# Staging buffers of a filter's first stage moved into an idle region, eight for one stream and five for the others

## The chip, the cores and the metric

One core of a Trainium2 chip runs the whole program. The metric is the device time of one execution in microseconds (us), the median of several runs. The engines are PE (matmuls; its weight loads are a row of their own, PEld), DVE (vector), ACT (activations and copies), POOL and SP; SP does nothing here but issue DMAs, and ACT issues some as well.

## The reference, cut to what matters

Two branches read the same normalized input. A is a long convolution over the sequence, done by FFT; B is a gated feed-forward net.

```python
xn = layernorm(q)                                # 2048 x 512
# A: short causal filter over k, times v, then a long filter per channel
kv = (sum over t of k_pad[t:t+S] * shift_k[:, 3-t]) * v
y  = irfft(rfft(pad(kv)) * rfft(pad(ssm_k)))[:S] + kv * ssm_D
s  = xn * y
# B
h  = gelu(xn @ w_gate) * (xn @ w_up)             # 512 -> 1792
g  = silu(h @ w_down)                            # 1792 -> 512
out = q + s * g
```

## The kernel before

**The branches.** B goes in four row groups q = 0 to 3 of 512 rows. A group has 14 units m (L971): a gate matmul group `tg` and an up group `tu` of four 128x512 matmuls each, a gelu on ACT into GE (L986) and a product on DVE into HT (L989). The down-projection `down(q)` (L992) makes four tiles jt of 14 matmuls each; the first of them is cut into three pieces, so that it can begin before all of HT is there. A tanh on ACT (L1004) and a DVE instruction (L1006) turn each tile into the gate G. XN, the normalized input, is computed on DVE (`ln(q)`, L739, beginning with `bn_stats` at L742) and for q > 0 transposed by DMAs that SP issues (L764).

**The filter.** A's FFT of length 4096 is two stages of matmuls with tables of sines. Between the stages the data go through DRAM, because the second stage needs them in another order. The first stage (`stage1`, L877) makes 16 tiles for the filter's own taps (stream H, from HTr, the transposed `ssm_k`) and later 16 for the products kv (stream K, from V). Each tile is two matmuls into a pair of PSUM banks, a copy by ACT (L563) into a staging buffer of the tile AST, and a store: H to the DRAM tensor ZH, issued by ACT; K to ZK, issued by SP. When all of ZH is stored, the second stage of H (L912 to L920) loads it in 16 parts (BH), multiplies, copies through AST with a scale (L917) and stores to ZS. When all of ZK is stored, the main loop (L1027) loads BK from ZK and HS from ZS, transforms, multiplies with the filter on DVE (L1044), transforms back and stores to ZI; the last loop reads ZI (BI) and finishes. The kv products are made on DVE by `kshift(i)` (L936), nine instructions for each of four groups. A table for the way back is transposed by one DMA on SP (L1019) after the first stage of K.

**The buffers.** AST has three slots, which H's stage 1, K's stage 1 and H's stage 2 share, each with a DMA semaphore of its own:

```python
AST = new("AST", [128, 3, 2, 512], BF16)                 # L410
pAST = Pool_("AST", 3)                                   # L530
a = B(f"A{x}{t}", pAST)                                  # L879, and L913 for stage 2
```

G (16 KB per partition) is written by the tanh instructions only; at the start the same bytes hold Hn, the loaded `ssm_k`, and from 8 KB on the four BH slots lie over them. HTr ends where KK, the loaded `k`, begins (`kk_at`). HS and, at the end, BI lie over KK; HB, BO and BK lie over V and the scratch of `kshift`. PSUM has eight banks: at most four at a time go to B's tiles (pool `psF`), and at most three pairs to A's (pool `psC`).

**The order.** Nothing is ordered by hand. A planner (`Sched.run`, L307) places tasks on engines by a model of their durations: it takes the engine that can start first and, among the tasks that can start there within 0.25 us, the one with the lowest `prio`. Loads are an engine of their own in this model (`LOAD_BW`), and stores by ACT count as a fixed time after issue (`STORE`, L27; used in L892). `after=` makes a task follow others in the plan. The instructions are then issued in the planned order, each engine's in sequence, and each waits on semaphores for what it touches (`Trk`, L51). So an instruction whose data come later than planned holds up what is queued behind it on its engine, SP's DMA issues included. Of the priorities, a lower number going first: copies of H 2, stage 1 of K 3, stage 2 of H on PE 5 (its copies 2.5), up groups 9 + q, gate groups 10 + q, whole down tiles and last pieces 8.5 + q, first pieces 11.1 + q, `ln` 2 for group 1, `kshift` 4, stores 0, transposes of XN -1, BH loads 0.5.

Of the kernel before, what the change touches and what calls it, by code (L numbers as in the profile page):

```python
# [6 lines left out]
BF16 = mybir.dt.bfloat16  # L7
# [16 lines left out]
N_WARM = 16  # L24
ORDER = "w1 k0 v0 w2 k1 v1 w3 d0 d1 k2 v2 x1 k3 v3 x2 x3"
NF_BANKS = 4
STORE = 3500.0  # L27
NC_PAIRS = 3


# [20 lines left out]
class Trk:  # L51
# [313 lines left out]
def act(n, sb=False):  # L365
    return 170.0 + n * 0.833 + (30.0 if sb else 0.0)
# [6 lines left out]
def build_kernel(nc, A_q, A_k, A_v, A_shift_k, A_ssm_k, A_ssm_D, B_w_gate, B_w_up, B_w_down, out):  # L373
    with ExitStack() as es0:
# [8 lines left out]
        def at(name, shape, dt, offset):  # L383
            return nc.alloc_sbuf_tensor_at(name, shape, dt, offset=offset)
# [61 lines left out]
        ZK = nc.dram_tensor("ZK", [NG, 128, DM], BF16, kind="Internal")  # L446
# [25 lines left out]
        def bank(b):  # L472
            return PSALL[:, 512 * b.slot:512 * (b.slot + 1)]
# [4 lines left out]
        def R_bank(b):  # L478
            return [R_ps[b.slot // 2][b.slot % 2]]
# [15 lines left out]
        R_AST = [res(f"AST{j}", AST[:, j, :, :]) for j in range(3)]  # L495
# [57 lines left out]
        def op(engs, fn, r=(), w=(), rr=(), ww=(), prio=5, lat=0.0, after=()):  # L553

            def emit(e):
                R = rr() if callable(rr) else rr
                W = ww() if callable(ww) else ww
                trk.op(e, lambda h: fn(e, h), r=R, w=W)
            return S.add(engs, emit, r=r, w=w, prio=prio, lat=lat, after=after)

        def copy(e, h, o, i):
            if e == "ACT":
                return h.activation(o, i, ACTF.Copy)  # L563
            return h.tensor_copy(o, i)

        def mm(h, o, l, r, st, sp):
            return h.matmul(o, lhsT=l, rhs=r, start=st, stop=sp)  # L567
# [30 lines left out]

        ZERO = AST[:, 0, 0, :]
        bwarm = B("warm")  # L600
        S.add([("DVE", 250.0)], lambda e: trk.op("DVE", lambda h: h.memset(ZERO, 0.0), w=[R_AST[0]]), w=[bwarm], prio=-9)
        warm = B("pswarm", pF)

        def warm_up(e):
            for i in range(N_WARM):
                trk.op("PE", lambda h: mm(h, bank(warm), ZERO[:, 0:128], ZERO, True, True), r=[R_AST[0]], w=R_bank(warm), accum=True)
# [266 lines left out]


        s1_tasks = {"H": [], "K": []}

        def stage1(x, t, data, R_data, b_data, Z, prio):  # L877
# [8 lines left out]
            op([("ACT", act(1024))], lambda e, h: copy(e, h, AST[:, a.slot, :, :].rearrange("p c d -> p (c d)"), ps(psl(p))),  # L886
               r=[p], w=[a], rr=lambda: R_ps[psl(p)], ww=lambda: [R_AST[a.slot]], prio=prio)

            def st(e):
                dst = bass.AP(Z, 2 * t * DM, [[32 * DM, 128], [DM, 2], [1, DM]])  # L890
                dma(e, dst, AST[:, a.slot, :, :], d_ast[a.slot], [R_AST[a.slot]], [R_Z[x][t]])
            S.add([("ACT" if x == "H" else "SP", 350.0)], st, r=[a], w=[bZ[x][t]], prio=0, lat=STORE if x == "H" else 0.0, nbytes=262144 if x == "K" else 0)  # L892

        d_ast = [dsem(f"d_ast{j}") for j in range(3)]
# [4 lines left out]
        def z_pair(Z, n):  # L899
            return bass.AP(Z, 2 * n * 128 * DM, [[DM, 128], [128 * DM, 2], [1, DM]])  # L900

        def fwd(p, T, R_T, buf):
            def f(e):
                s = psl(p)
                for i in range(2):
                    trk.op("PE", lambda h, i=i: mm(h, ps(s, i), MT[:, 0, :], T[:, buf.slot, i, :], True, True),
                           r=[R_MT, R_T[buf.slot]], w=[R_ps[s][i]], accum=True)
            return f

        d_bh = [dsem(f"d_bh{j}") for j in range(4)]  # L910
        h2_tasks = []
        for n in range(16):  # L912
            bh, p, a = B(f"bh{n}", pBH), B(f"psf{n}", pC), B(f"hf{n}", pAST)  # L913
            S.add([("SP", 350.0)], lambda e, n=n, bh=bh: dma(e, BH[:, bh.slot, :, :], z_pair(ZH, n), d_bh[bh.slot], R_Z["H"], [R_BH[bh.slot]]),
                  r=bZ["H"], w=[bh], prio=0.5, nbytes=262144, after=h_tr_tasks)
            h2_tasks.append(S.add([("PE", pe(2))], fwd(p, BH, R_BH, bh), r=[bMT, bh], w=[p], prio=5, lat=200.0))
            op([("ACT", act(1024))], lambda e, h, p=p, a=a: h.activation(AST[:, a.slot, :, :].rearrange("p c d -> p (c d)"), ps(psl(p)), ACTF.Copy, scale=2.0 ** -12),  # L917
               r=[p], w=[a], rr=lambda p=p: R_ps[psl(p)], ww=lambda a=a: [R_AST[a.slot]], prio=2.5)
            S.add([("SP", 350.0)], lambda e, n=n, a=a: dma(e, ZS[n], AST[:, a.slot, :, :], d_ast[a.slot], [R_AST[a.slot]], [R_Z["S"][n]]),
                  r=[a], w=[bZ["S"][n]], prio=0, nbytes=262144)  # L920


        kshift_tasks = []
# [40 lines left out]

        for i in range(4):
            kshift(i)
        for t in range(NT):
            stage1("K", t, V[:, t, :], R_V[t], [bKV[t // 4]], ZK, 3)

# [22 lines left out]
        def down(q):  # L992
            for jt in range(4):
                p = B(f"psd{q}_{jt}", pF)
                t = 4 * q + jt

                for m0, m1 in ((0, 4), (4, 9), (9, 14)):
                    def f(e, p=p, jt=jt, m0=m0, m1=m1):
                        for m in range(m0, m1):
                            trk.op("PE", lambda h, m=m: mm(h, bank(p), HT[:, q % 2, m, 128 * jt:128 * (jt + 1)], Wd[:, m, :], m == 0, m == MF - 1),  # L1000
                                   r=[R_HT[q % 2][m], R_Wd[m // 7]], w=R_bank(p), accum=True)
                    down_tasks[q].append(S.add([("PE", pe(m1 - m0))], f, r=(bHT[q] if jt else bHT[q][m0:m1]) + bWd[m0 // 7:(m1 + 6) // 7], w=[p], prio=9 + q - 0.5 if jt or m1 == MF else 11.1 + q, lat=200.0))
                bt = B(f"tanh{q}_{jt}")
                op([("ACT", act(512))], lambda e, h, t=t, p=p: h.activation(G[:, t, :], bank(p), ACTF.Tanh, scale=0.5), r=[p], w=[bt],  # L1004
                   rr=lambda p=p: R_bank(p), ww=[R_G[t]], prio=1, after=h_tr_tasks + (h2_tasks if q >= 2 else []))
# [150 lines left out]
```

## Time and profile before

| | us |
|---|---|
| median of 3 runs (lowest, highest) | 236.66 (236.32, 240.0) |
| the profiled execution | 235.92 |
| its span in the trace | 234.1 |
| PE busy | 209.5 |
| DVE busy | 169.8 |
| ACT busy | 121.5 |

Spans start with the first and end with the last instruction of the trace, so a profiled execution's own time is a little longer. Busy time of PE is modelled: a matmul that stands alone counts 0.38 us, one in a full row far less, so the count of matmuls in a stretch says more than the busy share. Issuing a DMA does not count as busy time of the engine that issues it; the rows ACTq and SPq show it. In a timeline, a row has start, duration, engine, line, operation, result and source, count, and in brackets the idle time before it with what ended it.

### The profile page before, as it was taken

To read this page: it belongs to the slowest core of one execution; us is meant where nothing else is said; L and a number is where in the kernel's file an instruction comes from. 1 tells how busy PE (TensorE), PEld (TensorE's weight loads), DVE (VectorE), ACT (ScalarE), POOL (GpSimd) and SP (SyncE) were. 2 spreads that over 40 slices of the span, in tenths; PEclk is the share of its full clock that TensorE was granted. 3 is DMA by queue.
4 is the path that set the end of the run, shared out by engine and by line. 5 is a ranking of instruction groups with operands and counts; after the bars stand their busy time and mean duration, and the time that the engine had idled before them with its cause. 6 is when DMAs were issued, how large, how long until landed. Compare 5 with 4: busy or idle time off the path is not lost.

```text
span 234.1 us, 2865 instructions
## 1 busy us (share of the span) xinstructions
PE 209.5 (89%) x979; PEld 92.3 (39%) x996; DVE 169.8 (73%) x250; ACT 121.5 (52%) x154; POOL 16.8 (7%) x43
## 2 busy tenths in 40 slices
PE   7599977899996989999969899999999999999990
PEld 2355432234442333443334344444344444444440
DVE  6978875968696879894014798988894646989535
ACT  2698575667966688876163255553434623131220
POOL 8632000010300000001000000000000000000000
PEclk9999999999999999999999999999999999999996
DMA  6999999956788888699797989999972267703402
GB/s 170 393 294 365 372 387 414 416 210 188 230 197 254 282 278 298 226 269 320 148 250 223 304 269 296 294 305 303 293 217 90 90 236 233 251 8 114 152 0 90
DMA packets 47617, 56.96 MB, mean 243 GB/s; under 512 B 13809, under 2 KB 31986, under 8 KB 47602
## 3 DMA queue, kind: packets, MB, share of 16 engines
q1 hardware_dynamic: 45298, 52.58, 71.6%
q10 hardware_dynamic: 2304, 4.20, 4.7%
q8 instruction: 8, 0.13, 0.2%
q14 instruction: 7, 0.06, 0.1%
HBM read 35.26 MB, written 18.87 MB: 231 GB/s over the span
## 4 chain that ended last, share of the span: by engine, by line
PE 51%; DMA 27%; ACT 11%; SPq 6%; issue 2%; DVE 2%; ACTq 0%
PE psall L567 49%; DMA ZH<-AST 11%; DMA ZK<-AST 5%; ACT AST L563 5%; DMA Hn<-in_A_ssm_k_dram 4%; DMA ZS<-AST 3%; DMA ZI<-BO 3%; SPq L1019 2%; SPq L544 2%; ACT AST L917 2%; DMA BK<-ZK 2%; SPq L764 2%; ACT GE L986 1%; PE psall L800 1%; ACT BO L563 1%
## 5 line engine op out<-in xcount | busy, mean ns | idle before, releaser
L567 PE MATMUL psall<-xnT,Wu 128*128 128x512 bf16 x224 | 56.4, 379 | 1.3 <-ACT AST L563 1.1
L989 DVE TENSOR_TENSOR HT<-psall,GE 128x512 bf16<-128x512 f32 x56 | 37.9, 686 | 26.6 <-PE psall L567 24.4
L986 ACT ACTIVATE GE<-psall 128x512 bf16<-128x512 f32 x56 | 33.4, 598 | 45.5 <-PE psall L567 43.9
L567 PE MATMUL psall<-xnT,Wg 128*128 128x512 bf16 x224 | 56.1, 379 | 0.3 <-ACT GE L986 0.3
L567 PE MATMUL psall<-Wd,HT 128*128 128x512 bf16 x219 | 51.4, 379 | 2.7 <-ACT AST L917 2.4
L1044 DVE TENSOR_TENSOR HB<-psall,HS 128x1024 bf16<-128x1024 f32 x32 | 36.9, 1216 | 10.0 <-PE psall L567 10.0
L563 ACT ACTIVATE AST<-psall 128x1024 bf16<-128x1024 f32 x32 | 32.5, 1025 | 11.3 <-DMA ZH<-AST 5.9
L567 PEld LDWEIGHTS psall<-Wd,HT 128*128 128x128 bf16 x224 | 21.9, 98 | 29.0 <-ACT AST L917 2.8
L567 PEld LDWEIGHTS psall<-xnT,Wu 128*128 128x128 bf16 x224 | 21.3, 98 | 28.1 <-ACT AST L563 1.7
L567 PEld LDWEIGHTS psall<-xnT,Wg 128*128 128x128 bf16 x224 | 21.6, 98 | 26.9 <-ACT GE L986 1.2
L1006 DVE SCALAR_TENSOR_TENSOR G<-G,psall 128x512 bf16<-128x512 bf16 x16 | 10.5, 682 | 20.9 <-ACT G L1004 20.9
L563 ACT ACTIVATE BO<-psall 128x1024 bf16<-128x1024 f32 x16 | 16.4, 1023 | 14.5 <-PE psall L567 12.2
L917 ACT ACTIVATE AST<-psall 128x1024 bf16<-128x1024 f32 x16 | 16.2, 1026 | 10.6 <-DMA ZK<-AST 5.9
L1004 ACT ACTIVATE G<-psall 128x512 bf16<-128x512 f32 x16 | 9.4, 597 | 18.1 <-PE psall L567 18.0
L567 PE MATMUL psall<-HB,MT 128*128 128x512 bf16 x62 | 16.0, 380 | 1.0 <-ACT BO L563 0.8
L958 DVE TENSOR_TENSOR KTM<-KK,SKB 128x2048 bf16<-128x2048 bf16 x12 | 14.6, 1218 | 0.1
L960 DVE TENSOR_TENSOR KAC<-KAC,KTM 128x2048 bf16<-128x2048 bf16 x12 | 14.6, 1217 | 0.1
L567 PE MATMUL psall<-BH,MT 128*128 128x512 bf16 x32 | 9.5, 381 | 3.3 <-DMA BH<-ZH 2.1
L567 PE MATMUL psall<-HTr,F 128*128 128x512 bf16 x29 | 8.6, 381 | 3.6 <-ACT AST L563 3.5
L749 POOL TENSOR_TENSOR mv<-mv,NHALF 128x4 f32<-128x4 f32 x4 | 5.4, 1338 | 84.1 <-DVE mv L748 84.1
L742 DVE BATCH_NORM_STATS2 stats<-X 128x6 f32<-128x512 bf16 x16 | 10.4, 671 | 0.9 <-DMA X<-in_A_q_dram 0.9
L1084 DVE TENSOR_TENSOR XN<-psall,XN 128x1024 bf16<-128x1024 f32 x8 | 9.6, 1216 | 0.7 <-PE psall L567 0.7
(73 smaller groups left out, 139.8 us busy)
## 6 DMA issues: line engine op xcount, KB each, us to landing
ZH<-AST ACTq DMA_DIRECT2D x16, 256.0 KB, 5.6
ZK<-AST SPq DMA_DIRECT2D x16, 256.0 KB, 2.6
BH<-ZH SPq DMA_DIRECT2D x16, 256.0 KB, 3.5
ZS<-AST SPq DMA_DIRECT2D x16, 256.0 KB, 2.9
HS<-ZS SPq DMA_DIRECT2D x16, 256.0 KB, 5.4
HS<-ZS SPq DMA_DIRECT2D x32, 128.0 KB, 5.1
BK<-ZK SPq DMA_DIRECT2D x16, 256.0 KB, 4.8
ZI<-BO SPq DMA_DIRECT2D x16, 256.0 KB, 4.6
```

What stands on the lines that cost most here:

```text
L563: return h.activation(o, i, ACTF.Copy)
L567: return h.matmul(o, lhsT=l, rhs=r, start=st, stop=sp)
L742: op([("DVE", 670.0)], lambda e, h, t=t: h.bn_stats(stats[:, t, :], X[:, t, :]), r=[bX[q][t % 4 // 2]], w=[bst[t]], rr=[R_X[t]], ww=[R_st[ ...
L917: op([("ACT", act(1024))], lambda e, h, p=p, a=a: h.activation(AST[:, a.slot, :, :].rearrange("p c d -> p (c d)"), ps(psl(p)), ACTF.Copy, ...
L958: op([("DVE", dur)], lambda e, h, j=j, m=m: h.tensor_tensor(KTM[:, m.slot, :, :], kk(j), sk(j), ALU.mult), r=need + [bSKB, a], w=[m], rr=l ...
L960: op([("DVE", dur)], lambda e, h, m=m: h.tensor_tensor(KAC[:, a.slot, :, :], KAC[:, a.slot, :, :], KTM[:, m.slot, :, :], ALU.add), r=[m], ...
L986: op([("ACT", act(512))], lambda e, h: h.activation(GE[:, g.slot, :], bank(pg), ACTF.Gelu_apprx_tanh), r=[pg], w=[g], rr=lambda: R_bank(pg ...
L989: op([("DVE", dve(512, 1))], lambda e, h: h.tensor_tensor(HT[:, q % 2, m, :], bank(pu), GE[:, g.slot, :], ALU.mult), r=[pu, g], w=[bHT[q][m]],
L1004: op([("ACT", act(512))], lambda e, h, t=t, p=p: h.activation(G[:, t, :], bank(p), ACTF.Tanh, scale=0.5), r=[p], w=[bt], rr=lambda p=p: R_ ...
L1006: op([("DVE", dve(512, 1))], lambda e, h, t=t, p=p: h.scalar_tensor_tensor(out=G[:, t, :], in0=G[:, t, :], scalar=1.0, in1=bank(p), op0=AL ...
L1044: op([("DVE", dve(1024, 1))], lambda e, h, k=k, pk=pk, qq=qq, hs=hs: h.tensor_tensor(HB[:, qq.slot, :, :].rearrange("p c d -> p (c d)"), p ...
L1084: op([("DVE", dve(1024, 1))], lambda e, h, p=p, xs=xs: h.tensor_tensor(xs, ps(psl(p)), xs, ALU.mult), r=[p], w=[bS[j], bXN[2 * j], bXN[2 * ...
```

## The change

H's stage 1 gets eight staging slots of its own, ASH, laid over G. The three slots of AST and two new ones, ASX, are left to K's stage 1 and H's stage 2 together. ASX lies over 2 KB of HTr's end and 2 KB of KK's beginning; HS and BI move up by 2 KB, and HB, BO and BK down by 1 KB. The copies of H now follow the transposes of `ssm_k` (over whose source ASH lies), the copies of K follow H's stage 1 and the first `kshift`, and the tanh instructions follow the ZH stores. `STORE` goes from 3500 to 5000 ns. H's stage 2 stands behind `kshift` in the source, its BH loads follow the ZH stores, and its matmuls' priority goes from 5 to 10.5. The first pieces of the down-projection go from 11.1 + q to 10.05 + q. No work is added or taken away; the rest of the kernel is unchanged.

```diff
-STORE = 3500.0
+STORE = 5000.0
...
-        HS = at("HS", [128, 4, 2, 2, DM], BF16, kk_at)
-        place["at"] = kk_at + 19456
+        ASX = at("ASX", [128, 2, 2, DM], BF16, kk_at - 2048)
+        ASH = at("ASH", [128, 8, 2, DM], BF16, g_at)
+        HS = at("HS", [128, 4, 2, 2, DM], BF16, kk_at + 2048)
+        place["at"] = kk_at + 18432
...
-        BI = at("BI", [128, 8, 2, DM], BF16, kk_at)
+        BI = at("BI", [128, 8, 2, DM], BF16, kk_at + 2048)
+        ast = {"H": [ASH[:, j, :, :] for j in range(8)], "K": [AST[:, j, :, :] for j in range(3)] + [ASX[:, j, :, :] for j in range(2)]}
...
-        pAST = Pool_("AST", 3)
+        pAST = {x: Pool_("AST" + x, len(ast[x])) for x in "HK"}
...
         def stage1(x, t, data, R_data, b_data, Z, prio):
             p = B(f"ps1{x}{t}", pC)
-            a = B(f"A{x}{t}", pAST)
+            af = h_tr_tasks if x == "H" else s1_tasks["H"] + kshift_tasks[:1]
+            a = B(f"A{x}{t}", pAST[x])
...
-               r=[p], w=[a], rr=lambda: R_ps[psl(p)], ww=lambda: [R_AST[a.slot]], prio=prio)
+               r=[p], w=[a], rr=lambda: R_ps[psl(p)], ww=lambda: [R_AST[x][a.slot]], prio=prio, after=af)
...
+            if x == "H":
+                zh_tasks.append(t_st)
...
-            bh, p, a = B(f"bh{n}", pBH), B(f"psf{n}", pC), B(f"hf{n}", pAST)
+            bh, p, a = B(f"bh{n}", pBH), B(f"psf{n}", pC), B(f"hf{n}", pAST["K"])
...
-                  r=bZ["H"], w=[bh], prio=0.5, nbytes=262144, after=h_tr_tasks)
-            h2_tasks.append(S.add([("PE", pe(2))], fwd(p, BH, R_BH, bh), r=[bMT, bh], w=[p], prio=5, lat=200.0))
+                  r=bZ["H"], w=[bh], prio=0.5, nbytes=262144, after=zh_tasks)
+            h2_tasks.append(S.add([("PE", pe(2))], fwd(p, BH, R_BH, bh), r=[bMT, bh], w=[p], prio=10.5, lat=200.0))
...
-                    down_tasks[q].append(S.add([("PE", pe(m1 - m0))], f, r=(bHT[q] if jt else bHT[q][m0:m1]) + bWd[m0 // 7:(m1 + 6) // 7], w=[p], prio=9 + q - 0.5 if jt or m1 == MF else 11.1 + q, lat=200.0))
+                    down_tasks[q].append(S.add([("PE", pe(m1 - m0))], f, r=(bHT[q] if jt else bHT[q][m0:m1]) + bWd[m0 // 7:(m1 + 6) // 7], w=[p], prio=9 + q - 0.5 if jt or m1 == MF else 10.05 + q, lat=200.0))
...
-                   rr=lambda p=p: R_bank(p), ww=[R_G[t]], prio=1, after=h_tr_tasks + (h2_tasks if q >= 2 else []))
+                   rr=lambda p=p: R_bank(p), ww=[R_G[t]], prio=1, after=zh_tasks + (h2_tasks if q >= 2 else []))
```

More of the change, by code (lines that the diff above doesn't have):

```diff
@@ L494, in build_kernel @@
         R_GE = [res(f"GE{j}", GE[:, j, :]) for j in range(3)]
-        R_AST = [res(f"AST{j}", AST[:, j, :, :]) for j in range(3)]
+        R_AST = {x: [res(f"AST{x}{j}", a) for j, a in enumerate(ast[x])] for x in "HK"}
         R_G = [res(f"G{t}", G[:, t, :]) for t in range(NT)]
@@ L885, in stage1 @@
             s1_tasks[x].append(S.add([("PE", pe(2))], m, r=[bF1[t // 4]] + b_data, w=[p], prio=prio, lat=200.0))
-            op([("ACT", act(1024))], lambda e, h: copy(e, h, AST[:, a.slot, :, :].rearrange("p c d -> p (c d)"), ps(psl(p))),
-               r=[p], w=[a], rr=lambda: R_ps[psl(p)], ww=lambda: [R_AST[a.slot]], prio=prio)
+            op([("ACT", act(1024))], lambda e, h: copy(e, h, ast[x][a.slot].rearrange("p c d -> p (c d)"), ps(psl(p))),
+               r=[p], w=[a], rr=lambda: R_ps[psl(p)], ww=lambda: [R_AST[x][a.slot]], prio=prio, after=af)
@@ L889, in st @@
             def st(e):
                 dst = bass.AP(Z, 2 * t * DM, [[32 * DM, 128], [DM, 2], [1, DM]])
-                dma(e, dst, AST[:, a.slot, :, :], d_ast[a.slot], [R_AST[a.slot]], [R_Z[x][t]])
-            S.add([("ACT" if x == "H" else "SP", 350.0)], st, r=[a], w=[bZ[x][t]], prio=0, lat=STORE if x == "H" else 0.0, nbytes=262144 if x == "K" else 0)
-        d_ast = [dsem(f"d_ast{j}") for j in range(3)]
+                dma(e, dst, ast[x][a.slot], d_ast[x][a.slot], [R_AST[x][a.slot]], [R_Z[x][t]])
@@ L895, in build_kernel @@
+            t_st = S.add([("ACT" if x == "H" else "SP", 350.0)], st, r=[a], w=[bZ[x][t]], prio=0, lat=STORE if x == "H" else 0.0, nbytes=262144 if x == "K" else 0)
+            if x == "H":
+                zh_tasks.append(t_st)
+        d_ast = {x: [dsem(f"d_ast{x}{j}") for j in range(len(ast[x]))] for x in "HK"}
         for t in range(NT):
             stage1("H", t, HTr[:, t, :], R_HTr[t], [bHTr[k][t // 8] for k in range(KD)], ZH, 2)
-        def z_pair(Z, n):
-            return bass.AP(Z, 2 * n * 128 * DM, [[DM, 128], [128 * DM, 2], [1, DM]])
@@ L966, in build_kernel, with z_pair, fwd, f @@
             kshift(i)
+        def z_pair(Z, n):
+            return bass.AP(Z, 2 * n * 128 * DM, [[DM, 128], [128 * DM, 2], [1, DM]])
+        def fwd(p, T, R_T, buf):
+            def f(e):
+                s = psl(p)
+                for i in range(2):
+                    trk.op("PE", lambda h, i=i: mm(h, ps(s, i), MT[:, 0, :], T[:, buf.slot, i, :], True, True),
+                           r=[R_MT, R_T[buf.slot]], w=[R_ps[s][i]], accum=True)
+            return f
+        d_bh = [dsem(f"d_bh{j}") for j in range(4)]
+        h2_tasks = []
+        for n in range(16):
+            bh, p, a = B(f"bh{n}", pBH), B(f"psf{n}", pC), B(f"hf{n}", pAST["K"])
+            S.add([("SP", 350.0)], lambda e, n=n, bh=bh: dma(e, BH[:, bh.slot, :, :], z_pair(ZH, n), d_bh[bh.slot], R_Z["H"], [R_BH[bh.slot]]),
+                  r=bZ["H"], w=[bh], prio=0.5, nbytes=262144, after=zh_tasks)
+            h2_tasks.append(S.add([("PE", pe(2))], fwd(p, BH, R_BH, bh), r=[bMT, bh], w=[p], prio=10.5, lat=200.0))
+            op([("ACT", act(1024))], lambda e, h, p=p, a=a: h.activation(ast["K"][a.slot].rearrange("p c d -> p (c d)"), ps(psl(p)), ACTF.Copy, scale=2.0 ** -12),
+               r=[p], w=[a], rr=lambda p=p: R_ps[psl(p)], ww=lambda a=a: [R_AST["K"][a.slot]], prio=2.5, after=kshift_tasks[:1])
+            S.add([("SP", 350.0)], lambda e, n=n, a=a: dma(e, ZS[n], ast["K"][a.slot], d_ast["K"][a.slot], [R_AST["K"][a.slot]], [R_Z["S"][n]]),
+                  r=[a], w=[bZ["S"][n]], prio=0, nbytes=262144)
         for t in range(NT):
```

20 lines of the change are left out of this document (3 added, 17 removed).

## Prediction

> **What bounds the kernel now.** I read the stretches of the span first, because PE's share of the whole hides where it stands still. The columns are stretch, length, then busy time and instruction count of PE, weight loads, DVE, ACT and POOL, the granted clock, the DMA share and GB/s.
>
> ```profile
> 24.00:54.00 30.00, 25.01 (x110) 10.06 (x111) 22.27 (x32) 18.73 (x23) 1.05 (x1) 1.00 0.92 345
> 54.00:66.00 12.00, 11.84 (x55) 5.22 (x55) 9.14 (x23) 10.04 (x12) 1.91 (x1) 1.00 0.80 244
> 66.00:90.00 24.00, 20.47 (x91) 8.35 (x91) 19.94 (x22) 17.57 (x22) 0.00 (x0) 1.00 0.82 249
> 90.00:108.00 18.00, 17.78 (x81) 7.47 (x80) 15.24 (x25) 13.23 (x18) 1.01 (x1) 1.00 0.83 276
> 108.00:132.00 24.00, 20.12 (x90) 8.37 (x91) 7.00 (x11) 10.42 (x15) 0.00 (x0) 1.00 0.88 228
> 132.00:226.00 94.00, 92.73 (x423) 41.49 (x429) 71.83 (x83) 34.18 (x46) 0.00 (x0) 1.00 0.66 206
> ```
>
> From 132 to 226 us PE does nothing but work: 429 weight loads in 94.00 us, one matmul per 0.219 us. So only idle time of PE before 132 us can be won. I measure it with that pitch and the weight-load counts, since an isolated matmul's modelled busy time flatters PE: 24 to 54 us needs 111 x 0.219 = 24.3 of 30 us, 5.7 idle; 66 to 90 needs 19.9, 4.1 idle; 108 to 132 also 19.9, 4.1 idle; 90 to 108 has 0.5 and 54 to 66 none. That is 14.4 us, the most that any reordering could give.
>
> Next I asked what holds the staging buffers, the tile AST:
>
> ```profile
> its engine sat idle before it (us, times) until:
>   DMA ZK<-AST: 7.1, 3
>   DMA ZH<-AST: 5.9, 7
> ...
>   DMA ZS<-AST: 3.4, 5
> ...
> who waited for it (us, times):
> ...
>   PE psall L567: 9.5, 10
> ```
>
> ACT stood 16.4 us before its copies out of PSUM because the store of a slot's earlier content had not landed, and PE stood 9.5 us behind those copies. All three streams (ZH, then ZK and ZS) share three slots. The timeline of ACT shows the ring turning, and ACT's groups from 22.8 to 57 us (last two rows) sum the stage:
>
> ```profile
> 23.88 0.34 ACTq L544 DMA_DIRECT2D ZH<-AST  x1
> 24.27 1.02 ACT L563 ACTIVATE AST<-psall 128x1024 bf16<-128x1024 f32 x1 [0.42 <-PE psall L567]
> 25.70 1.02 ACT L563 ACTIVATE AST<-psall 128x1024 bf16<-128x1024 f32 x1 [0.41 <-PE psall L567]
> ...
> 29.48 1.02 ACT L563 ACTIVATE AST<-psall 128x1024 bf16<-128x1024 f32 x1 [1.75 <-DMA ZH<-AST]
> ...
> 56.64 0.33 ACTq L544 DMA_DIRECT2D ZH<-AST  x1
> ...
> L563 ACT ACTIVATE AST<-psall 128x1024 bf16<-128x1024 f32 x16 | 16.4, 1022 | 7.6 <-DMA ZH<-AST 5.9 <-PE psall L567 0.8 <-ACT AST L563 0.8
> L986 ACT ACTIVATE GE<-psall 128x512 bf16<-128x512 f32 x11 | 6.6, 597 | 4.5 <-PE psall L567 2.9 <-ACT AST L563 1.6
> ```
>
> The store issued at 23.88 lets the fourth copy start at 29.48, 5.6 us later.
>
> **First stage, ZH on eight slots.** The ring wait goes: 5.9 us of ACT. It does not all become time, because ACT is nearly full itself. Two copies with the store issue between them lie 25.70 - 24.27 = 1.43 us apart; 16 of them and 11 gelus of 0.6 us are 22.9 + 6.6 = 29.5 us, against 34.1 us taken (22.83, where the first copy starts, to 56.97, when the last issue is over). So ACT allows 4.6 us. PE had 5.7 us idle there; while ACT is full, PE must fill with matmuls that need no copy, which is what the down-projection pieces are. I take 4.2 us; bounds 0 and 4.6.
>
> Would eight slots wait for stores as well? The stage's stores, by DMA queue (q1 is SP's, q10 ACT's), with the load of X that the next step needs (DMA view from 24 to 36 us; the last row from 32.1 to 32.6 us):
>
> ```profile
> DMA packets 3793, 4.58 MB, mean 381 GB/s; under 512 B 164, under 2 KB 3002, under 8 KB 3792
> q1 hardware_dynamic: 3216, 3.52, 84.7%
> q10 hardware_dynamic: 576, 1.05, 23.1%
> ZH<-AST ACTq DMA_DIRECT2D x6, 256.0 KB, 5.9
> ...
> X<-in_A_q_dram SPq DMA_DIRECT2D x1, 512.0 KB, 11.1
> ```
>
> At a landing time of 5.9 us and a unit plus a filter tile every 2.15 us (10 matmuls at 0.219), about three stores are in the air; eight slots hold even if a store takes 15 us. The engines are full: 381 GB/s. [...]
>
> **A new wait, X1.** The planner counts loads as one engine of their own, untouched by stores, so it will still place the first statistics of the second row group as early as now:
>
> ```profile
> 32.19 0.49 SPq L544 DMA_DIRECT2D X<-in_A_q_dram  x1
> ...
> 45.90 0.69 DVE L742 BATCH_NORM_STATS2 stats<-X 128x6 f32<-128x512 bf16 x1
> ...
> 54.45 5.54 SPq L764 DMA_TRANSPOSE xnT<-XN  x4
> ...
> 69.73 1.89 PE L567 MATMUL psall<-xnT,Wg 128*128 128x512 bf16 x8
> ```
>
> X1 lands at 32.19 + 11.1 = 43.3 us and is used at 45.90: 2.6 us to spare. In the changed kernel some three more stores of 0.262 MB land before it, 0.79 MB / 0.381 = 2.1 us, while DVE, no longer held by PE, arrives up to 4 us sooner. Queued behind that instruction on DVE are the HT products, which free PE's gate banks; four banks (two units) cover about 1.7 us. I charge 1.0 us, bounds 0 and 3. The transposed XN (issued from 54.45 to 59.99) is needed at 69.73 now; 4.2 us earlier still leaves some 5 us, so it costs nothing unless the loads slip by more than that.
>
> **Middle and late, ZK and ZS on five slots.** Three rows for the gap at 72 us, the rest for the one at 112 us:
>
> ```profile
> 65.35 5.16 SPq L764 DMA_TRANSPOSE xnT<-XN  x4
> 70.55 1.08 SPq L544 DMA_DIRECT2D BH<-ZH  x2
> ...
> 73.68 0.59 PE L567 MATMUL psall<-BH,MT 128*128 128x512 bf16 x2 [2.06 <-DMA BH<-ZH]
> ...
> 110.31 5.15 SPq L764 DMA_TRANSPOSE xnT<-XN  x4
> ...
> 115.52 0.59 SPq L544 DMA_DIRECT2D ZK<-AST  x1
> 117.11 5.45 SPq L1019 DMA_TRANSPOSE G<-F  x1
> 117.85 1.02 ACT L917 ACTIVATE AST<-psall 128x1024 bf16<-128x1024 f32 x1 [5.92 <-DMA ZK<-AST]
> 118.93 3.19 PE L567 MATMUL psall<-Wd,HT 128*128 128x512 bf16 x14 [2.35 <-ACT AST L917]
> 123.72 0.46 SPq L544 DMA_DIRECT2D ZK<-AST  x1
> 126.35 3.96 SPq L544 DMA_DIRECT2D BK<-ZK  x7
> 130.68 0.59 PE L567 MATMUL psall<-BK,MT 128*128 128x512 bf16 x2 [0.76 <-DMA BK<-ZK]
> ```
>
> At 72 us SP is shut for 5.16 us by four transposes, the BH load waits behind them, and PE waits 2.06 us for it. The change leaves the transposes alone, so about 2 of the 4.1 us stay. ZH will be complete some 4 us earlier, and the second transform now gives way to the up halves and the down-projection (priority 10.5 for 5), so PE can have other work there. I take 1.0 us, bounds 0 and 4.1. At 112 us, too, SP is shut (5.15 us, then 5.45 us for the table transpose), but here three slots make it a stop: a ZK store sits behind the transposes until 115.52, ACT can copy nothing until 117.85, PE can't get its bank until 118.93, and the last ZK store, and so the first BK load, slips to 126.35. With five slots two more copies can be done before the ring is full. Earlier in the stretch the ring stops limiting the flow: the 32 copies for ZK and ZS then have five slots to turn in, so fewer of them are left when SP shuts. I take 2.6 us, bounds 0 and 4.1. After 132 us PE is full in either case, so an earlier BK load wins nothing beyond the gap.
>
> **What moves at no cost.** The 64 store and load DMAs keep their number, queue and size; ASH lies in G, whose first tanh comes at 62.87 (row below), after the last ZH issue at 56.64, and its four banks cover PE for 12 us of down-projection; without that cover a tanh would hold a bank for one landing, 5.9 us. HS, HB, BO, BK and BI move by 1 to 2 KB over K and V tiles that are dead by then.
>
> ```profile
> 62.87 1.09 ACT L1004 ACTIVATE G<-psall 128x512 bf16<-128x512 f32 x2
> ```
>
> **Sum.** 4.2 - 1.0 + 1.0 + 2.6 = 6.8 us off the profiled execution's 235.92 us (its span 234.1 and 1.82 around it): 229.1. That execution lies 0.74 us below the median of the three runs, 236.66, so I forecast **229.9 us**, 2.9% less; its own range with the other cases left out is 227 to 232.
>
> **Rivals.** *Only the first ring matters.* The late gap is made by SP's transposes; if the planner again leaves ZS and ZK stores behind them, five slots fill as three did. Gain 4.2 - 1.0 = 3.2: 233.5 us. For it: 10.6 us of blocked SP at 110 to 122.6. Against it: the chain there is visibly one of slots.
>
> *Nearly all idle time goes.* 4.6 + 4.1 + 4.1 of the three gaps with no new wait, about 11.5 in practice: 225.2 us. Against it: ACT's fullness and the unchanged transposes.
>
> *The stores don't get faster.* If q10 keeps its share (1.05 MB in 12 us, 3 us per store), sixteen stores need 48 us however many slots there are; then slots fill, ZH ends no earlier than now, and only some 0.5 us is won: 236.2. Against it: three stores in the air at 5.9 us each are 3 x 0.262 / 5.9 = 0.133 MB per us, half more than that mean, so the queue was not the limit while the slots were being refilled. [...]
>
> *The stores win and the loads lose* (the other side). If all nine stores that now land after X1 go ahead of it, X1 comes 9 x 0.262 / 0.381 = 6.2 us later, at 49.5. DVE, in order, stands there from about 43.3, where it lands now; after 1.7 us PE stands too, 4.5 us. The second group's XN slips by 6.2 and PE, 4.2 us early, needs it at 65.5: the 7 us of slack (transposes over at 60, plus landing, against 69.73) shrink to nothing and some 3 us more are lost; the K products on the same DVE slip too, so the late gap gains nothing. 235.92 - 4.2 + 4.5 + 3 = 239.2, with the 0.74: 240 us, from 236 to 244. It decides once X1 lands after about 48 us. Against it: at 43 us only about nine of sixteen copies exist now, and copies are limited by ACT at 1.43 us each.
>
> **How the numbers follow.** Forecast 0.48, nearly all idle 0.08, only the first ring 0.29, stores no faster 0.06, loads late 0.09. Two per cent, 4.7 us, is about what a measurement of this kernel can tell from no change. Below 231.9: the forecast and the case under it, 0.56. Above 241.4: the worse part of the last, 0.04. Between: 0.40. The range 225.5 to 237.0 leaves out half of the all-idle case and most of the last, some 0.12; its ends are the bounds of the terms (all taken at their best gives 224 us, none but a small gain 236).
>
> **What would show it.** Right: waits of ACT for ZH under 1 us instead of 5.9; the last ZH issue near 52 us; PE's idle time from 24 to 54 us at 1 to 3 us instead of 5.7; waits for ZK and ZS together well under 10.5 us; the first BK load before 120 us; PE full from there on. The X1 charge shows as DVE's first statistics waiting on the DMA of X. Wrong: a first stage as long as before, landing times of ZH above 10 us, or the gap around 112 us still ended by a copy that waits for a store; and if PE's idle time is gone before 132 us but the end doesn't move, the reading that PE is full afterwards is wrong.

## The result, and the profile after

The changed kernel takes **229.64 us** (median of four executions, 228.98 to 230.02) against 236.62 us of the kernel before beside it: a ratio of 0.9706, with a 95% interval of 0.9672 to 0.974. The profiled execution took 228.98 us with a span of 227.2; before it was 235.92 with 234.1. (The ratios leave out executions over 1.5% slower than the fastest of their kernel, the medians do not; two profiles further down, those of K on three slots and of the transposes on ACT's queue, are of such executions.) The stretches of the changed kernel, with the same columns as before:

```profile
24.00:54.00 30.00, 29.18 (x132) 12.35 (x132) 26.52 (x42) 21.86 (x28) 1.04 (x1) 1.00 1.01 363
54.00:66.00 12.00, 11.82 (x54) 5.17 (x54) 9.38 (x16) 8.79 (x11) 1.92 (x1) 1.00 0.84 221
66.00:90.00 24.00, 21.44 (x95) 8.89 (x96) 21.91 (x24) 21.78 (x28) 0.00 (x0) 1.00 0.91 299
90.00:108.00 18.00, 17.39 (x78) 7.47 (x79) 11.20 (x22) 12.55 (x16) 1.01 (x1) 1.00 1.03 334
108.00:132.00 24.00, 21.55 (x91) 8.94 (x90) 13.71 (x15) 7.80 (x11) 0.00 (x0) 0.93 1.02 263
132.00:219.00 87.00, 86.46 (x397) 39.19 (x402) 65.05 (x78) 31.05 (x44) 0.00 (x0) 1.00 0.56 181
```

The kernel before, in the last of these stretches:

```profile
132.00:219.00 87.00, 85.73 (x391) 38.35 (x397) 69.86 (x81) 32.98 (x44) 0.00 (x0) 1.00 0.71 219
```

Read the weight loads (the second count), which say how far the program has come. With one per 0.216 us (402 in 87 us), the difference in each stretch is time won: 24 to 54 us 132 for 111, **4.5 us**; 66 to 90 us 96 for 91, 1.1; 108 to 132 us 90 for 91, **nothing**; 132 to 219 us 402 for 397, 1.1. The stretches 54 to 66 and 90 to 108 give back 0.2 each, the start loses 0.4 (132 loads for 134 before 24 us), and the end wins 0.4. With the 0.2 lost at 108 that makes 6.1 of the 6.9 us by which the spans differ. The rest is the way of counting: a load that lies across a border counts in both stretches, so the stretches before add up to 1000 loads and those after to 996, though each trace holds 996. So one figure of a stretch is good to a load or so, 0.2 us.

The staging tile of H in the changed kernel: its instructions, what ACT waited for before its copies, and the landing times of its stores.

```profile
L566 ACT ACTIVATE ASH<-psall x16: 1018/1018/1023, 23.3 to 51.2; 128x1024 bf16<-128x1024 f32 x16
L547 ACTq DMA_DIRECT2D ZH<-ASH x16: 326/326/347, 24.3 to 52.3; - x16
its engine sat idle before it (us, times) until:
  ACT ASH L566: 1.3, 3
  PE psall L570: 0.8, 2
...
DMA to landing us min/median/max: 3.7/6.3/7.4
```

No copy waits for a store any more, where ACT had stood 5.9 us for ZH. The last store of ZH is issued at 52.28 instead of 56.64. No copy into the five slots of K and ZS waited for a store either, where 10.5 us had gone to those two. ACT's groups from 22.8 to 53 us:

```profile
L566 ACT ACTIVATE ASH<-psall 128x1024 bf16<-128x1024 f32 x16 | 16.3, 1020 | 2.1 <-ACT ASH L566 1.3 <-PE psall L570 0.8
L993 ACT ACTIVATE GE<-psall 128x512 bf16<-128x512 f32 x11 | 6.6, 597 | 5.9 <-PE psall L570 5.9
```

The stage runs from 23.26 to 52.61 us, 29.35 us, close to the floor of 29.5 us that the prediction gave ACT. But PE is full as well: in the middle of the stage, one unit's gelu follows the other after 2.16 us, which is ten matmuls at 0.216 us, and waits for PE:

```profile
39.18 0.60 ACT L993 ACTIVATE GE<-psall 128x512 bf16<-128x512 f32 x1 [0.65 <-PE psall L570]
...
41.34 0.60 ACT L993 ACTIVATE GE<-psall 128x512 bf16<-128x512 f32 x1 [0.65 <-PE psall L570]
```

Part of each such wait is the store issue of 0.33 us that stands on ACT before the gelu; the rest is ACT waiting. The DMA view from 24 to 36 us shows the 16 engines as busy as before (a DMA share of 1.08 in both kernels), and what each queue moved:

```profile
DMA packets 3796, 4.55 MB, mean 379 GB/s; under 512 B 157, under 2 KB 2959, under 8 KB 3795
q1 hardware_dynamic: 3130, 3.31, 80.8%
q10 hardware_dynamic: 665, 1.23, 26.7%
```

ACT's queue q10 moved 1.23 MB instead of 1.05, SP's q1 3.31 instead of 3.52, at 379 GB/s in all instead of 381: the stores gained bytes and the loads lost them, but only 0.2 MB in 12 us. The load of X (its time to landing last) and its first use:

```profile
31.30 0.43 SPq L547 DMA_DIRECT2D X<-in_A_q_dram  x1
43.85 0.69 DVE L745 BATCH_NORM_STATS2 stats<-X 128x6 f32<-128x512 bf16 x1 [0.84 <-DMA X<-in_A_q_dram]
...
X<-in_A_q_dram SPq DMA_DIRECT2D x1, 512.0 KB, 12.5
```

X is issued 0.9 us earlier than before and takes 12.5 us instead of 11.1, so it lands at 43.8 us (43.3 before); DVE is there at 43.0, 2.9 us earlier than before, and waits 0.84 us. Now the late gap, with the first BK load and the end of the stop (timelines of SP and PE put together in order of time), and the granted clock behind it (columns of the second view: stretch, length, PE busy, clock, DMA share, GB/s):

```profile
103.38 0.58 SPq L547 DMA_DIRECT2D ZK<-AST  x1
...
105.72 5.15 SPq L767 DMA_TRANSPOSE xnT<-XN  x4
110.97 3.08 SPq L547 DMA_DIRECT2D BK<-ZK  x6
114.00 1.76 PE L570 MATMUL psall<-BK,MT 128*128 128x512 bf16 x4 [2.28 <-DMA BK<-ZK]
114.10 6.38 SPq L1026 DMA_TRANSPOSE G<-F  x1
115.55 4.48 PE L570 MATMUL psall<-Wd,HT 128*128 128x512 bf16 x14
119.87 1.03 PE L570 MATMUL psall<-HB,MT 128*128 128x512 bf16 x4
```

```profile
114.00:115.00 1.00, 0.88 (x3) 0.87 1.03 298
115.00:116.00 1.00, 1.00 (x4) 0.50 0.64 200
116.00:117.00 1.00, 1.00 (x4) 0.50 0.89 295
117.00:118.00 1.00, 1.00 (x4) 0.50 1.56 317
118.00:119.00 1.00, 1.00 (x5) 0.92 1.00 161
```

The last ZK store leaves SP at 103.38 instead of 123.72 and the first BK load at 110.97 instead of 126.35. Yet PE stands as long as before, for another reason: not a slot, but BK itself, whose load had to wait on SP until four transposes were issued. The stop of 2.28 us is followed by about 3.5 us in which PE gets half its clock: the 18 matmuls from 114.00 to 119.87 take 5.87 us, where 18 x 0.216 = 3.9 would do. The stop costs 2.3 us directly and the clock 2.0 more, nearly all of the 4.6 us that are idle in this stretch.

### The profile page after: what moved, and what is told of

Same layout as the page of the kernel before. It is cut to its first block, busy times and chain, and to the rows that moved or that the text cites. A ratio compares the mean times of both kernels' runs of the same rounds, so it can differ in the third digit from the quotient of the medians.

```text
span 227.2 us, 2878 instructions
## 1 busy us (share of the span) xinstructions
PE 210.3 (93%) x979; PEld 94.7 (42%) x996; DVE 170.1 (75%) x250; ACT 120.9 (53%) x154; POOL 16.8 (7%) x43
## 4 chain that ended last, share of the span: by engine, by line
PE 70%; ACT 12%; DMA 7%; DVE 5%; SPq 2%; issue 2%; ACTq 1%
PE psall L570 69%; ACT AST L566 2%; ACT ASH L566 2%; SPq L767 2%; ACT GE L993 2%; DMA ZK<-ASX 1%; DMA BK<-ZK 1%; DMA X<-in_A_q_dram 1%; DMA BH<-ZH 1%; DMA ZK<-AST 1%; DVE stats L745 1%; DVE G L1013 1%; ACT F L652 1%; ACT xnT L566 1%; ACT ASX L566 1%
## 5 line engine op out<-in xcount | busy, mean ns | idle before, releaser
L570 PE MATMUL psall<-xnT,Wu 128*128 128x512 bf16 x224 | 55.6, 379 | 0.4 <-ACT ASH L566 0.4
L570 PE MATMUL psall<-xnT,Wg 128*128 128x512 bf16 x224 | 55.1, 379 | 0.8 <-ACT ASX L969 0.4
L566 ACT ACTIVATE ASH<-psall 128x1024 bf16<-128x1024 f32 x16 | 16.3, 1020 | 2.1 <-ACT ASH L566 1.3
L566 ACT ACTIVATE AST<-psall 128x1024 bf16<-128x1024 f32 x12 | 11.8, 1021 | 0.8 <-PE psall L570 0.8
L570 PE MATMUL psall<-BK,MT 128*128 128x512 bf16 x31 | 9.3, 396 | 2.5 <-DMA BK<-ZK 2.3
```

## The experiments

**The theory** after seeing this: eight slots for H are worth the 4.5 us before 54 us by themselves. Five slots for K and ZS do take the slot waits away, but what is freed runs into SP, shut by its own transposes. **The rivals:** that only one of the rings matters at all; and that the new priorities, which move work on PE, did it and not the slots. In all ratios below the kernel before was run beside the experiment on the same chip. Unless the kernel before is named as the base, an experiment keeps the rest of the change: `STORE`, the new `after=` rules, the later place of H's stage 2 in the source.

**Each ring put back, and the priorities put back.** In the changed kernel, first K's five slots to three:

```diff
-ast = {..., "K": [AST[:, j, :, :] for j in range(3)] + [ASX[:, j, :, :] for j in range(2)]}
+ast = {..., "K": [AST[:, j, :, :] for j in range(3)]}
```

> The changed kernel, but K's stage 1 and H's stage 2 share three staging slots as before instead of five; H keeps its eight. Theory after reading the two traces: the eight H slots brought most of the 7 us and the five slots about 2, so 231 to 232 us (changed kernel 229.6), waits of ACT for ZK and ZS stores back at several us, and the K stores late again. By the terms of the prediction the five slots are worth 1.0 + 2.6 = 3.6 us: 233.2. If the new priorities do the work and not the slots: 229.6.

Then H's eight to three of its own (`range(8)` to `range(3)` for ASH, the five of K kept):

> The changed kernel, but H's stage 1 has three slots of its own instead of eight; the five slots for K and H's stage 2 stay. Theory: the first ring is worth about 4.5 us, so 234 us, with PE's idle time from 24 to 54 us back at 5 to 6 us and ACT's waits for ZH at about 6 us. By the terms of the prediction (4.2 - 1.0) 232.8. If the new priorities do the work: 229.6.

Then both rings as changed, but the priorities as before:

```diff
-... prio=10.5          # second transform of H on PE
+... prio=5
-... else 10.05 + q     # first pieces of the down-projection
+... else 11.1 + q
```

> The changed kernel with the two old priorities (H's stage 2 on PE at 5 instead of 10.5, the first pieces of the down-projection at 11.1 + q instead of 10.05 + q); all slots stay. Theory: the slots carry the gain, so 229 to 230.5 us. Rival: without the down-projection pieces ahead, PE has no filler while ACT is full in the first stage, and H's stage 2 takes PSUM pairs early: 232 to 233 us.

Measured: K on three slots 232.65 us, ratio 0.977 [0.9673, 0.9868]; H on three 231.47, 0.976 [0.9678, 0.9841]; old priorities 235.73, **0.9919** [0.9874, 0.9964]. Putting either ring back alone costs little (0.6 and 0.5%, small beside the intervals), so the theory's 234 us for H on three was too much, and its 229 to 230.5 for the old priorities too little. With H on three slots the early loss returns, but it is wholly made up by 108 us, as the stretches 24 to 54 and 54 to 108 us of that kernel show (the changed kernel: 132, then 229):

```profile
24.00:54.00 30.00, 26.40 (x116) 10.36 (x116) 24.32 (x35) 21.09 (x27) 1.05 (x1) 1.00 0.88 328
54.00:108.00 54.00, 53.46 (x244) 24.04 (x248) 44.38 (x67) 42.64 (x53) 2.93 (x2) 1.00 0.92 287
```

248 loads in 54 us is a full PE (54 / 0.216 = 250): work that was not done early fills what would have been idle later. By 108 us this kernel has 364 loads, the changed one 361, the one before 337. What it loses, it loses after that. The old priorities cost 5 us (0.9919 against 0.9706) although they bring back no slot wait. SP's late order in that kernel shows a large part of why:

```profile
106.14 6.88 SPq L1026 DMA_TRANSPOSE G<-F  x1
113.07 5.19 SPq L767 DMA_TRANSPOSE xnT<-XN  x4
118.38 6.84 SPq L547 DMA_DIRECT2D BK<-ZK  x8
121.23 1.03 PE L570 MATMUL psall<-BK,MT 128*128 128x512 bf16 x2 [5.48 <-DMA BK<-ZK]
```

Here the planner put both transposes, 12 us of SP, ahead of the BK loads, and PE stood 5.48 us and then ran at half clock (0.50 from 121 to 125 us, and five matmuls in 2.34 us up to 127). By weight loads, 18 of the 32 by which its profile lies behind the changed kernel's at 132 us are lost there. The other 14 are lost from 54 to 108 us, some of them in a stretch of half clock from 89.6 to 93 us (0.81 from 89 to 90 us, then 0.50); why PE falls behind there was not tested. So the priorities matter in good part through the place of two transposes in SP's order, and not through waits for slots.

**Single parts alone, with a control.** Eight slots for H with three for K and the old priorities; five for K with three for H and the old priorities; the two priorities alone in the kernel before; and the changed kernel once more. The first two join edits shown above; the third is

```diff
-... prio=5
+... prio=10.5
-... else 11.1 + q
+... else 10.05 + q
```

> The changed kernel itself once more, as the control for the three below, since the first four runs had a kernel before of 237.6 us and noisier times. Both theories: 0.97 of the kernel before.

> One part alone: eight slots for H's stage 1; K and H's stage 2 keep three slots, and the two priorities are the old ones. If the eight slots carry the gain (the terms of the prediction: 4.2 - 1.0 us): 0.985 of the kernel before, some 3 us less. If the stop of PE before the first BK load decides, with the half clock behind it, then the 4.5 us won by 54 us are waited away there, because the K stores still end behind SP's transposes: 0.995 to 1.0, with PE waiting 4 us or more for BK.

> One part alone: five slots for K and H's stage 2; H's stage 1 has three slots of its own, and the two priorities are the old ones. By the terms of the prediction (1.0 + 2.6 us) 0.985 of the kernel before. If the stop before the first BK load decides: the first BK load is issued some 8 to 12 us earlier than 126 us, but PE has less done by then; 0.98 to 0.99, with the wait for BK at 2 to 4 us.

> One part alone: the kernel before with its one ring of three slots and only the two new priorities (H's stage 2 on PE at 10.5, the first pieces of the down-projection at 10.05 + q). If the slots carry the gain: 1.0 of the kernel before. If the priorities do the work by themselves, as leaving them out cost 5 us in the run with all slots: 0.98. With three slots I expect little, since ACT's waits for slots stay: 0.99 to 1.0.

Measured: control 230.29 us, 0.9702 [0.9673, 0.973]; eight H alone 231.76, **0.9735** [0.9679, 0.9792]; five K alone 232.9, 0.9806 [0.9766, 0.9846]; priorities alone 239.38, 1.0095 [1.0065, 1.0125]. The parts do not add: eight H alone give 2.65%, five K alone 1.9%, both without the priorities 0.8%, with them 3.0%. That the priorities did it by themselves falls, since alone they lose 1%; but with both rings most of the gain hangs on them. That only the first ring matters can't be upheld either, since the kernel with five K slots alone wins 1.9%; how much of that the five slots win and how much the rest of the change is not shown, since no run has three and three slots with that rest. Eight slots for H did better than either figure expected of them and come within the error of the whole change. In that kernel the slot waits of K stay, and a copy ends PE's late stop as in the kernel before (waits of PE and ACT):

```profile
PE psall L570 <- ACT AST L969: 3.8, 3, 2.6
...
ACT AST L969 <- DMA ZS<-AST: 4.2, 1, 4.2
```

Why the parts don't add shows in the progress of PE. From the profiles, one execution each: weight loads by stretch, first BK load, and the longest late wait of PE:

| kernel | 24–54 | 54–108 | 108–132 | sum | first BK | longest late wait of PE, us |
|---|---|---|---|---|---|---|
| before | 111 | 226 | 91 | 428 | 126.35 | 2.4, a copy |
| changed | 132 | 229 | 90 | 451 | 110.97 | 2.3, BK |
| changed again (control) | 133 | 230 | 85 | 448 | 112.72 | 2.9, BK |
| K on three | 134 | 233 | 73 | 440 | 120.03 | 4.6, BK |
| H on three | 116 | 248 | 84 | 448 | 114.20 | 3.3, BK |
| old priorities | 132 | 215 | 72 | 419 | 118.38 | 5.5, BK |
| eight H only | 134 | 227 | 95 | 456 | 122.22 | 2.6, a copy |
| five K only | 117 | 242 | 80 | 439 | 114.73 | 3.3, BK |
| priorities only | 107 | 227 | 76 | 410 | 124.55 | 5.4, BK |

Every kernel with eight H slots has 132 to 134 loads from 24 to 54 us, every other 107 to 117. But by 108 us one of the rings is enough: 361 with eight H alone, 359 with five K alone, 361 with both, against 337 and 334 without. (The kernel with old priorities is the exception, with 347.) Each of the two wins the same 5 us, one early, the other while PE catches up; so the theory's "by themselves" holds for H, and nothing here shows that the second ring adds to the first. The last stretch, 72 to 95 loads, follows neither ring. It goes with the wait of PE for BK or for a copy; two executions of the changed kernel differ by five loads there.

**BK ahead of the transposes.** In the changed kernel, `xnT(3)` and the table transpose are made to follow the first six BK loads in the plan:

```diff
+if n < 6:
+    for t in xt_tasks[8:12] + [t_g1]:
+        t.deps.append(t_bk)
```

> The changed kernel, with the last four transposes of XN and the table transpose placed behind the first six BK loads on SP. Theory: PE's stop of 2.3 us near 112 us and the half clock of some 3.3 us behind it come from the BK loads that wait on SP behind 5.2 us of transposes; with the loads first, the first BK load is issued near 106 us, the stop and the half clock go, and the time falls by 2 to 3.5 us to 226 to 227.6. Rival: PE's work before the last row group is fixed, so the stop only moves to where that group's gate matmuls wait for their transposed XN: 229 to 230.

Measured: 231.73 us, 0.9763 [0.9701, 0.9825], no faster than the changed kernel. BK goes at 108.23, no matmul waits for it, the clock stays at 1.00. But the transposes now stand before the ZI stores on SP (5.15 us from 112.90, 5.50 from 120.37), and ACT waits for these stores before it can copy into BO (13.4 us in all, 4.9 in the changed kernel):

```profile
128.42 2.11 ACT L566 ACTIVATE BO<-psall 128x1024 bf16<-128x1024 f32 x2 [5.39 <-DMA ZI<-BO]
129.50 1.04 PE L570 MATMUL psall<-BK,MT 128*128 128x512 bf16 x4 [3.65 <-ACT BO L566]
```

The stop was only moved, though not to the gate matmuls that the rival of this run named; what this kernel loses, it loses after 132 us (386 loads to 219 us, 402 in the changed kernel), where PE stops three times more for 0.85 to 0.91 us, twice for copies into BO. This points to the shutting of SP itself. Three kernels follow it up.

**The late transposes on ACT's queue.**

```diff
-trk.dma("SP", ... xnT, transpose=True)          S.add([("SP", 350.0)], ...)
+trk.dma("ACT" if q == 3 else "SP", ...)         S.add([("ACT", 1290.0) if q == 3 else ("SP", 350.0)], ...)
-S.add([("SP", 350.0)],  ... G1, F1, transpose=True ...)
+S.add([("ACT", 5450.0)], ... after=xt_tasks[8:12])
```

> The changed kernel with the late transposes taken off SP's queue: the four of xnT(3) and the table transpose are issued by ACT (counted at 1.29 and 5.45 us in the plan), so that SP goes from the ZK and HS DMAs straight to the BK loads. Theory (the stop at 112 us is SP being shut by transposes, and the half clock behind it follows from the stop): no wait of PE for BK over 0.5 us, clock 1.00 from 108 to 132 us, SP's BK loads from about 108 on with no gap, and ratio 0.955 to 0.963 to the kernel before (about 227 us). Rival (ACT can't spare 10 us there either: its copies and tanhs hold the PSUM banks while it stands at a transpose, so the stop is merely moved, as it was when the transposes were put behind the BK loads): PE waits 3 to 5 us for ACT's copies or tanhs between 105 and 130 us, ratio 0.968 to 0.98.

Measured: 230.52 us in one execution and 235.23 to 236.49 in three others, so no ratio stands. SP does go straight on (BK from 108.79), and PE waits 1.14 us for BK instead of 2.28 (under 0.5 was expected). But ACT is shut, 5.83 us for the four of `xnT(3)` and for the table far longer than SP had been:

```profile
112.91 14.49 ACTq L1027 DMA_TRANSPOSE G<-F  x1
129.02 1.03 PE L570 MATMUL psall<-BK,MT 128*128 128x512 bf16 x2 [5.88 <-ACT BO L566]
```

In this profile the rival of the run was right: ACT can't spare the time, and the stop moved again, to a copy into BO, and is longer than the rival's 3 to 5 us.

**The table transpose in pieces,** with and without giving `xnT(3)` its true duration and a place behind the stores:

```diff
-S.add([("SP", 350.0)], ... G1[:], F1[:], transpose=True ..., prio=8)
+for i in range(4):      # rows 4i to 4i + 3 each
+    S.add([("SP", 1370.0)], ... G1[:, ts], F1[:, ts], transpose=True ..., prio=8)
 and, in the second kernel only, xnT(3):
-S.add([("SP", 350.0)], ..., prio=-1)
+S.add([("SP", 1290.0)], ..., prio=0.45)
```

> The changed kernel with only the table transpose cut into four DMAs with their true cost in the plan; xnT(3) is left at 0.35 us and first in line. Theory of unbroken shutting: the wait for BK behind xnT(3) stays (2 to 3 us, it is ended before the table comes), the one behind the table goes; ratio 0.962 to 0.97. Rival (sum of SP's work): no gain, 0.968 to 0.975.

> The changed kernel with the table transpose cut into four DMAs (1.37 us each in the plan) and xnT(3) counted at 1.29 us with priority 0.45 for -1, all still on SP. Theory (what costs is the unbroken shutting of SP, not the transposes' sum): the BK loads and ZI stores pass between the pieces, PE's waits for BK and for ACT's copies behind ZI stores from 108 to 132 us fall from 3 to 5 us together to under 1.5, clock 1.00, ratio 0.957 to 0.965. Rival (each piece costs SP as much as the whole, or the sum of SP's work, ten us of transposes and the loads, is what sets BK's arrival): four pieces take over 8 us, the waits stay at 3 us or more, ratio 0.97 or above.

Measured: the pieces alone 229.57 us, 0.9666 [0.9581, 0.9751], which can't be told from the changed kernel's own; BK still waits behind `xnT(3)` (5.28 us on SP), PE 3.0 us for BK, clock 0.93 from 108 to 132 us. Both edits: **225.15 us, 0.949** [0.9427, 0.9554], clear of the changed kernel and better than expected. SP in the faster kernel, and its last stretch:

```profile
107.54 1.23 SPq L767 DMA_TRANSPOSE xnT<-XN  x1
108.89 3.06 SPq L547 DMA_DIRECT2D BK<-ZK  x6
112.05 1.21 SPq L767 DMA_TRANSPOSE xnT<-XN  x1
113.30 1.15 SPq L547 DMA_DIRECT2D BK<-ZK  x2
114.49 2.52 SPq L767 DMA_TRANSPOSE xnT<-XN  x2
...
130.30 1.87 SPq L1027 DMA_TRANSPOSE G<-F  x1
```

```profile
108.00:132.00 24.00, 23.54 (x110) 10.30 (x108) 17.50 (x19) 9.90 (x13) 0.00 (x0) 1.00 1.07 304
```

The same transposes, issued one or two at a time between loads and stores, and the table's after 130 us: PE waits 0.3 us for BK, the clock stays full, and there are 108 weight loads where the changed kernel had 90. That is 18 x 0.216 = 3.9 us, for 3.5 us less span (223.7); some 2 us of it is the shorter wait for BK and as much the clock. The sum of SP's work is not less: the four pieces take 1.87 and three times 1.32 us, 5.8 in all, against 6.38 for the whole in the changed kernel and 5.45 in the kernel before. So the rival, SP's sum of work, falls. What cost the time was the place of the transposes and that each group stood there in one block; no run separates the two. The pieces alone win nothing while `xnT(3)` stays in one block ahead of BK; moving `xnT(3)` with the table left whole was not run. The pieces also differ in the plan by more than their number: the planner charges a DMA at least its bytes at 350 per ns, so the whole table counted 3.0 us of SP, not the 0.35 that its line names, and 2.5 us more until it landed. The pieces carry no byte count and are charged 5.5 us together and no landing.

**The same two edits in the kernel before:**

> The kernel before (three shared slots, old priorities) with only the two edits that made the fastest kernel: the table transpose in four pieces at 1.37 us, xnT(3) counted at 1.29 us with priority 0.45, behind the stores. Theory (two separate losses: the first stage's slots, 4.5 us before 54 us, which the change ends, and SP shut at 105 to 122 us, which it doesn't): the weight loads by 54 us stay at 107 to 112, ACT's waits for ZH at 5 to 7 us, and the late stop shrinks; ratio 0.975 to 0.982. Rival A (with three slots the late stop is the ring's own: stores land too late whatever SP does): waits of ACT for ZK and ZS stay near 10 us and PE's stop near 2 us, ratio 0.985 to 1.0. Rival B (the late stop was the whole matter and the early idle time is caught up anyway): 0.95 to 0.965.

Measured: 233.98 us, 0.9886 [0.982, 0.9951], outside the theory's range and inside rival A's. The stretches:

```profile
24.00:54.00 30.00, 24.72 (x111) 10.15 (x110) 22.12 (x32) 18.28 (x23) 1.04 (x1) 1.00 0.90 339
66.00:90.00 24.00, 20.67 (x86) 8.23 (x85) 18.56 (x21) 16.59 (x20) 0.00 (x0) 0.93 0.77 237
108.00:132.00 24.00, 23.17 (x107) 10.00 (x106) 9.33 (x14) 11.38 (x17) 0.64 (x1) 1.00 1.00 257
```

The early stretch stays as it was (110 loads, ACT's waits for ZH 5.9 us). The late stop goes (106 for 91, 3.2 us), although slots still make ACT wait 7.8 us for ZK and ZS, so rival A has the number without the mechanism. In between 1.3 us are lost (85 for 91): PE stops 2.05 us for BH at 74.09 as the kernel before does (2.06 us, clock 1.00 behind it), but here half clock follows it (0.65, 0.50, 0.50 and 0.65 in the four us from 74). Two losses, then, and the edits that take one leave the other; against the changed kernel the same edits are worth twice as much (0.949 against 0.9702). How much of that comes from the clock in this one profile is open.

## Why the prediction was right, and where it was not

The total, 229.9 us, came within 0.3 us, and most of the signs it named came true. Its terms did not all come with it, and that they sum to the right total is luck.

- **First stage, +4.2: right.** The ring wait is gone, the last issue came at 52.28 ("near 52"), and the stage took what the prediction's floor for ACT allows. That floor was not the only limit: PE, with ten matmuls in 2.16 us, was full at nearly the same pace. PE's idle time fell from 6.0 to 1.5 us, within the 1 to 3 us named. What no step saw is that the kernel with five K slots alone has as many loads by 108 us.
- **The new wait, X1, −1.0: right in kind, too large.** X took 1.4 us longer, not 2.1, and landed only 0.5 us later because it was issued 0.9 us earlier. ACT's queue q10 took 0.18 MB more in those 12 us, where the prediction reckoned with 0.79 before X lands. That the whole of those 0.79 MB would come out of the loads was the author's estimate, and no run shows it; what the runs show is q1 with 0.21 MB less. DVE waited 0.84 us, and the stage's 4.5 us are measured with that wait in it.
- **Middle, +1.0: right,** 1.1 measured. PE's wait for BH behind SP's transposes stayed and shrank from 2.06 to 1.21 us.
- **Late, five slots, +2.6: wrong.** The step "three slots make it a stop" was true of the kernel before, and the slot waits did go, all 10.5 us of ACT. But the stop did not, and PE was not full behind the first BK load: measured −0.2 us. Behind the slots stood SP's transposes, which hold BK as they held ZK (5.15 us for the four of `xnT(3)` in both kernels); in the kernel with BK moved ahead the wait for BK goes, and in the one with single transposes the stop goes. The prediction had this as its rival "only the first ring matters", by ZS and ZK left behind the transposes; the place was right, the queued transfer another (BK).
- **"After 132 us PE is full in either case": wrong by 1.1 us.** The pitch of 0.219 us that the prediction took for full held some idle time, among it two waits for copies into BO (0.58 us at 169.87 and 0.25 at 183.50); a full PE runs at 0.216. The term was zero and should have been about 1. An earlier BK load is not shown to be the cause: from 132 to 219 us the kernel with the priorities alone has 400 loads with BK at 124.55, the one with five K slots alone 396 with BK at 114.73. The cause stays open.
- **Priorities as fillers only: wrong.** They lose 1% alone (1.0095) but are worth 2% with both rings (0.9919 against 0.9702), since they shift the plan, and with it SP's transposes among other things. The sum had no term for that, and the range needed one.

So the sum came out right by errors that cancel: −2.8 us in the late term met +1.3 in the first stage with X1, +0.1 in the middle, +1.1 after 132 us, and 0.4 in the small stretches and the loads counted twice.

The rival in which the loads lose fell at its condition: X landed at 43.8 us, far from the 48 from which it was to decide. That of stores no faster fell too: over the sixteen stores the median landing time is 6.3 us, 5.6 before, but no copy waits for one, and all sixteen are issued by 52.3 us.

The clock was in no step. Stops of 2.28 us (changed kernel) and 2.05 us (the two edits in the kernel before) were followed by about 3.5 us near half clock; stops of 2.35 us (before, 116.6 to 118.9), 2.06 us (before), 2.88 us (control) and 3.65 us (BK moved ahead, 125.9 to 129.5, clock 1.00 to 136 us) were not. So the length of the stop alone did not decide in these runs, and they give no threshold.

## What to carry to other kernels

When a stop is ended by a slot, look at what else is queued behind the same work before counting it as won: here the next transfer stood behind the same transposes. A planner whose cost for an instruction is a third of the truth (0.37 us, from its bytes, for a transpose that held its queue 1.29 us, a quarter of 5.15) can turn an edit of order or priority into a gain or a loss that no sum foresees, as the priorities here did. True costs, with pieces small enough to pass between, won 2% on top of the slots, and 1% without them. Take buffers' early and late effects apart by counting work done at fixed times, since time won early is often only used up later.

## What the runs showed of the hardware

- A DMA transpose held the queue that issued it: on SP 1.21 to 1.26 us for a single one of 128x512, 5.15 to 5.95 us for four in a row, and 5.2 to 7.1 us for the table. On ACT's queue the four took 5.83 us, and the same table transpose held ACT 14.49 us, with SP's loads and stores running beside it (one execution).
- Cut into four, that transpose held SP about as long in all (5.8, 6.5 and 6.3 us in the three kernels that have the pieces, 5.2 to 7.1 whole), and other DMAs passed between the pieces (in the fastest kernel ten of them, 5.4 us of SP, between the first two).
- Half clock came after a stop of 2.05 us in one run and not after 3.65 us in another. In the kernel with the old priorities it came after three short stops in a row (0.42, 1.09 and 0.52 us, ending at 89.57): eight matmuls then took 3.58 us, where 1.89 is usual. What decides it is left open.
